# Linear attention into a mish layer: one more group in seven products, and decayed keys on GpSimd

## The chip, the cores and the metric

The kernel runs on one core of a Trainium2 chip. The metric is the device time of one execution in microseconds. The kernel before takes 207.13 us (median of three runs, 207.11 to 207.51).

## What is computed

Two stages follow one another: a causal linear attention with a decay for each head, and a two-layer block with a mish activation. In the reference, cut to what matters:

```python
# q, k, v: (4, 8, 768, 64); lam: (8,); w_in: (512, 2048); w_out: (2048, 512)
for b in range(nb):                              # blocks of 64 positions
    intra = (q_b @ k_b^T * Dmask) @ v_b          # Dmask: lam^(i-j) for i >= j, else 0
    inter = (q_b * lam^(pos+1)) @ kv_state
    out_b = intra + inter
    kv_state = lam^64 * kv_state + (k_b * lam^(63-pos))^T @ v_b
x = out as (3072 tokens, 512)
h = x @ w_in
g = h * tanh(log(1 + exp(h)))                    # mish
return g @ w_out                                 # (3072, 512) float32
```

Inputs and output are float32; the kernel works in float16 with float32 sums.

## The kernel before

The kernel uses blocks of 128 positions, so the sequence of 768 gives six groups, numbered 0 to 5 in the code; "fourth group" is number 3. A group holds the same 128 positions of all four batches: 512 tokens. Three things are done for a group: its attention (batch by batch, b = 0 to 3), its first layer (x by w_in, then mish into `hsg`), and its second layer (`hsg` by w_out, stored).

The order of all instructions is written out by hand (a manual schedule), one list for each engine, and each engine takes its list in order. The middle of the kernel is a loop over periods n = 1 to 4. Period n does the second layer of group n in fourteen halves, called by `h(1)`; the first layer of group n + 1; and the attention of group m = n + 2 as long as there is one. So the keys of groups 3 and 4 are decayed in periods 1 and 2; in period 3, group 5, the last, needs no state and so no decayed keys.

The attention of a batch has two calls. `s_(b)` does the decayed keys `kd` (`decay_k`, L244: keys by `lk`) and the scores on TensorE (L251), masked on VectorE into `sb` (L255). `o_(b)` does the outputs on TensorE (L271, L276), scaled on VectorE into `xn` (L279) and transposed by a DMA into `xt`; then the state: products of `kd` and values on TensorE (L297), added to the old state on VectorE into `raw` (L305), and decayed on GpSimd into the new state `w` (L307). `fetch` has GpSimd issue the loads of the next group (L87).

The first layer is done in one of two ways, by a letter in `KINDS[n]` for each of its four parts. A "p" part is four plain units, `u(ni)`: four matmuls of 512 columns each (L324), then mish (L330). An "s" part is a set: one step of Strassen's scheme, which gets four quarter blocks from seven products (`seven`, L407) of four matmuls of 256 columns. It needs sums of w_in (`w_sum`, L370, four operations for each set, called by `ws(n, i)` through the table `WSUMS`), sums of x (`x_sums`, L385), two copies on ScalarE (L421, L429) and two additions on VectorE (L432, L436, the second into `c22`). Its steps are m1, seed, m2, m5, m6, m7, m3 and m4; `settle()` runs the m4 that `closing` left owed. The second layer has its own sums of `hsg` (`sums`, `gsum`, L481) on VectorE. The tile `kd` has three buffers; `kn`, `qn` and `vn` have four.

Of the kernel before, what the change touches and what calls it, by code (L numbers as in the profile page):

```python
# [20 lines left out]
def kernel(  # L21
# [10 lines left out]
    nc = tc.nc  # L32
# [209 lines left out]
    def decay_k(n, b, eng):  # L242
        kd[n, b] = work.tile([128, H, D], F16, name="kd", tag="kd", bufs=3)
        eng.tensor_tensor(out=kd[n, b], in0=kn[n, b], in1=bc(lk, 2, D), op=ALU.mult)  # L244
# [549 lines left out]
    def h(m=1):  # L794
        for _ in range(m):
            halves.pop(0)()
# [2 lines left out]

    KINDS = {1: "pppp", 2: "pppp", 3: "ssss", 4: "ssss"}
    WSUMS = {(1, 0): (0,), (1, 1): (2,), (2, 0): (1,), (2, 1): (3,)}

    for n in range(1, NG - 1):
        m = n + 2
        last = m >= NG - 1

        def u(*units):
            for ni in units:  # L810
                unit(n + 1, ni, next_bank())

        def s_(b):
            if m < NG:
                if not last:
                    decay_k(m, b, nc.vector)
                scores(m, b)

        def o_(b):
# [10 lines left out]
        def ws(n, i):  # L830
            for x in WSUMS.get((n, i), ()):
                for t in range(4):
                    w_sum(x, t, nc.vector)

        kinds = KINDS[n]
        sets = []
# [72 lines left out]
        if kinds[0] == "s":  # L909
            h(1)  # L910
            mm(0, "m2", "m5", "m6")
            sums(n, 1, 0, 1)
            h(1)
            o_(0)
            fetch(("k", 0), ("q", 0))
            closing(0)
        else:
            u(0)
            sums(n, 1, 0, 1)
            if n == 1:  # L920
                weight_sum(3, 0)
                weight_sum(3, 1)
            h(1)
            u(1)
            h(1)
            u(2)
            o_(0)
            fetch(("k", 0), ("q", 0))
            u(3)


        opening(1)
        h(1)
        if kinds[1] == "s":
            settle()
            mm(1, "m2")
            h(1)
            mm(1, "m5", "m6")
            sums(n, 1, 2)
            h(1)  # L940
            o_(1)
            fetch(("v", 0), ("k", 1))
            closing(1)
        else:
            u(8)
            settle()
            s_(1)
            sums(n, 1, 2, 3)
            ws(n, 0)
            h(1)  # L950
            u(9, 10)
            o_(1)
            fetch(("v", 0), ("k", 1))
            h(1)
            u(11)


# [6 lines left out]
        if kinds[2] == "s":  # L964
            mm(2, "m2", "m5", "m6")
            o_(2)
            fetch(("q", 1), ("v", 1))
            h(1)
            closing(2)
            h(1)  # L970
            sums(n + 1, 0, 0, 1)
            h(1)
        else:
            u(4)
            settle()
            s_(2)
            u(5)
            ws(n, 1)
            h(1)
            u(6)  # L980
            o_(2)
            fetch(("q", 1), ("v", 1))
            h(1)
            sums(n + 1, 0, 0, 1)
            h(1)
            u(7)
# [3 lines left out]
        if kinds[3] == "s":  # L990
            h(1)
            mm(3, "m2", "m5")
            h(1)
            mm(3, "m6")
            o_(3)
            h(1)
            mm(3, "m7", "m3")
            owed.append(3)
            sums(n + 1, 0, 2, 3)
        else:  # L1000
            s_(3)
            h(1)
            u(12)
            settle()
            h(1)
            o_(3)
            u(13)
            sums(n + 1, 0, 2, 3)
            h(1)
            u(14)  # L1010
# [46 lines left out]
```

## Time and profile before

| what | value |
|---|---|
| median of three runs | 207.13 us |
| the profiled execution's own time | 207.71 us |
| its span, first to last instruction | 205.8 us |
| busy: PE (TensorE) | 195.8 us, 95% |
| busy: DVE (VectorE) | 142.5 us, 69% |
| busy: ACT (ScalarE) | 95.9 us, 47% |
| busy: POOL (GpSimd) | 70.7 us, 34% |
| kd on DVE (L244) | 20 times, mean 741 ns |
| state decay on POOL (L307) | 14 times, mean 1456 ns |
| granted TensorE clock | 0.995 |

All times are from one execution, taken by the hardware profiler. PE is the row of matmuls, PEld that of weight loads, which overlap it. A row of a timeline gives the start in us from the span's start, the length, the engine, the line of the kernel, the operation and "output<-inputs" with shapes; behind it, in brackets, stands the idle time of the engine ahead of the instruction and what ended it. "x4" at the end counts merged instructions. Matmuls are pipelined, so the distance between the starts of two groups tells more than a group's length, which contains the last one's run out of the array.

### The profile page before, as it was taken

The numbers are of one execution on the slowest core, as the hardware profiler recorded it, in microseconds if no ns is written. First come the engines' busy times: TensorE is split into PE (matmuls) and PEld (weight loads), VectorE is DVE, ScalarE is ACT, GpSimd is POOL, SyncE is SP. The second block draws the span as 40 slices with busy tenths as digits, with TensorE's granted clock in tenths as the row PEclk, the third lists the DMA queues.
The fourth block names the chain that finished last, engine by engine and source line by source line (L and its number), as shares of the span: only waits on it lengthen the run. The fifth ranks groups of instructions, "written<-read, shape, count | busy, mean of one in ns | idle before, by whom it ended". The sixth has DMA issues, their size and how long they took to land.

```text
span 205.8 us, 4537 instructions
## 1 busy us (share of the span) xinstructions
PE 195.8 (95%) x1879; PEld 145.1 (70%) x1879; DVE 142.5 (69%) x241; ACT 95.9 (47%) x170; POOL 70.7 (34%) x68
## 2 busy tenths in 40 slices
PE   7968998999999999999999999999999999999991
PEld 3755554688865556667666567668888988888891
DVE  6656749777766957779965779977588676269041
ACT  4674686648631115243255342255574474827300
POOL 7996553533272560744630744530000000000020
PEclk9999999999999999999999999999999999999998
DMA  9999999999969999799994399992212221003123
GB/s 130 133 168 206 163 181 157 175 207 185 136 117 147 242 135 211 109 126 103 196 226 99 77 133 135 191 245 65 56 26 76 62 69 54 2 0 105 51 102 102
DMA packets 109302, 26.24 MB, mean 128 GB/s; under 512 B 99426, under 2 KB 108770, under 8 KB 109282
## 3 DMA queue, kind: packets, MB, share of 16 engines
q0 software_dynamic: 77536, 13.37, 83.8%
q1 hardware_dynamic: 30704, 12.33, 28.2%
q10 hardware_dynamic: 1042, 0.26, 0.6%
q8 instruction: 14, 0.23, 0.4%
q14 instruction: 6, 0.05, 0.1%
HBM read 27.26 MB, written 6.29 MB: 163 GB/s over the span
## 4 chain that ended last, share of the span: by engine, by line
PE 78%; DMA 9%; POOL 8%; DVE 1%; ACT 1%; issue 1%; POOLq 0%; DVEq 0%; ACTq 0%
PE bG L518 15%; PE bH L518 13%; DMA qn<-in_q_dram 8%; PE bA L324 5%; PE bC L324 5%; PE bB L324 4%; PE bB L407 3%; PE bC L407 3%; PE be L251 3%; PE bB L350 3%; PE bA L407 2%; PE bA L350 2%; PE bC L350 2%; POOL win L96 2%; PE bz L276 2%; PE bz L271 2%
## 5 line engine op out<-in xcount | busy, mean ns | idle before, releaser
L307 POOL TENSOR_TENSOR w<-raw,lbm 128x512 f16<-128x512 f32 x14 | 20.4, 1456 | 53.0 <-DVE raw L305 49.9
L518 PEld LDWEIGHTS <-gsum 128*128 128x128 f16 x336 | 31.1, 98 | 5.1
L324 PEld LDWEIGHTS <-win 128*128 128x128 f16 x200 | 18.3, 98 | 14.6 <-issue 1.0
L518 PEld LDWEIGHTS <-hsg 128*128 128x128 f16 x240 | 23.3, 98 | 5.6
L255 DVE TENSOR_TENSOR sb<-be,dm 128x512 f16<-128x512 f32 x23 | 15.8, 686 | 15.0 <-PE bo L251 15.0
L600 POOL TENSOR_TENSOR c<-p,u 128x512 f32<-128x512 f32 x1 | 1.3, 1275 | 61.2 <-DVE p L599 61.2
L518 PE MATMUL bH<-tsum,gsum 128*128 128x256 f16 x160 | 20.4, 273 | 0.0
L279 DVE TENSOR_TENSOR xn<-bz,lq 128x512 f16<-128x512 f32 x20 | 13.7, 686 | 9.3 <-PE bz L276 9.3
L518 PE MATMUL bG<-wout,hsg 128*128 128x256 f16 x160 | 20.1, 273 | 0.0
L324 PE MATMUL bA<-xt,win 128*128 128x512 f16 (+2 forms) x72 | 17.6, 367 | 0.6 <-ACT xt L265 0.6
L330 ACT ACTIVATE hsg<-bA 128x512 f16<-128x512 f32 x17 | 10.2, 597 | 13.9 <-PE bA L324 13.9
L324 PE MATMUL bC<-xt,win 128*128 128x512 f16 x64 | 16.4, 379 | 0.0
L330 ACT ACTIVATE hsg<-bB 128x512 f16<-128x512 f32 x15 | 9.0, 598 | 14.6 <-PE bB L324 14.6
L255 DVE TENSOR_TENSOR sb<-bo,dm 128x512 f16<-128x512 f32 x23 | 15.6, 679 | 0.0
L324 PE MATMUL bB<-xt,win 128*128 128x512 f16 (+2 forms) x64 | 15.6, 366 | 0.0
L481 DVE TENSOR_TENSOR gsum<-hsg 128x1024 f16<-128x1024 f16 x20 | 14.9, 751 | 0.0
L330 ACT ACTIVATE hsg<-bC 128x512 f16<-128x512 f32 x16 | 9.6, 597 | 11.4 <-PE bC L324 11.3
L244 DVE TENSOR_TENSOR kd<-kn,lk 128x512 f16<-128x512 f16 x20 | 14.6, 741 | 0.0
L350 PEld LDWEIGHTS <-win 128*128 128x128 f16 x128 | 12.1, 98 | 1.8
L407 PEld LDWEIGHTS <-wsum 128*128 128x128 f16 x128 | 12.4, 98 | 1.4
L87 POOL DMA_DIRECT2D kn<-in_k_dram x10 | 11.8, 1182 | 2.8 <-PE bo L297 1.4
L87 POOL DMA_DIRECT2D vn<-in_v_dram x10 | 11.6, 1160 | 2.6 <-DMA win<-in_moe_w_in_dram 1.8
(161 smaller groups left out, 393.1 us busy)
## 6 DMA issues: line engine op xcount, KB each, us to landing
out_dram<-osum SPq DMA_DIRECT2D x23, 256.0 KB, 2.4
kn<-in_k_dram POOLq DMA_DIRECT2D x11, 256.0 KB, 7.3
qn<-in_q_dram POOLq DMA_DIRECT2D x11, 256.0 KB, 6.8
vn<-in_v_dram POOLq DMA_DIRECT2D x10, 256.0 KB, 8.1
wout<-in_moe_w_out_dram POOLq DMA_DIRECT2D x4, 512.0 KB, 15.9
win<-in_moe_w_in_dram POOLq DMA_DIRECT2D x3, 512.0 KB, 11.5
vz<-in_v_dram POOLq DMA_DIRECT2D x2, 256.0 KB, 6.5
k<-in_k_dram SPq DMA_DIRECT2D x1, 256.0 KB, 3.3
```

The source lines that it names most:

```text
L87: nc.gpsimd.dma_start(out=tile_, in_=rows(src, n, 2 * bp, 2))
L244: eng.tensor_tensor(out=kd[n, b], in0=kn[n, b], in1=bc(lk, 2, D), op=ALU.mult)
L251: nc.tensor.matmul(p_[t][:, j, :], kT[n, b][rs, j, :], qT[n, b][rs, j, :], start=True, stop=True)
L255: nc.vector.tensor_tensor(out=sb[n, b, t], in0=p_[t], in1=dm[:, t], op=ALU.mult)
L279: nc.vector.tensor_tensor(out=xn, in0=po, in1=bc(lq, 2, D), op=ALU.mult)
L307: decay = lambda: eng.tensor_tensor(out=w_new, in0=raw, in1=lbm, op=ALU.mult)
L324: nc.tensor.matmul(open_[n, ni][:, lo:hi], win[ni // 4][:, kc, (ni % 4) * 128 : (ni % 4) * 128 + 128], xt[n][:, kc, lo:hi], start=(opens a ...
L330: nc.scalar.activation(h_tile(n)[:, ni, :], open_.pop((n, ni)), AF.Mish)
L350: nc.tensor.matmul(t[:, u, :], win[ni // 4][:, kc, m : m + 128], xt[n][:, kc, cs], start=(u == 0 and kc == 0), stop=(kc == NKC - 1), skip_ ...
L407: nc.tensor.matmul(t[:, u, :], lhs, rhs, start=(fresh and u == 0 and kk == 0), stop=(kk == 1), skip_group_check=True)
L481: nc.vector.tensor_tensor(out=gsum[n, i][:, ks, :], in0=a, in1=b, op=op)
L518: nc.tensor.matmul(t, lhs(kk, blk), rhs(kk)[:, lo:hi], start=(fresh and kk == 0), stop=(kk == HK - 1), skip_group_check=True)
```

## The change

Three edits go together.

First, period 2's letters become "ssss": the first layer of group 3 is done in four sets, as that of groups 4 and 5 is already. Group 2's stays plain.

Second, the sums of w_in, which were made two sets in period 1 and two in period 2, are all made in period 1, and the places of the calls in the plain branch move. (The calls in that branch run in period 1 alone now.)

Third, `decay_k` inside the loop goes from VectorE to GpSimd: eight operations, four in each of periods 1 and 2.

```diff
-    KINDS = {1: "pppp", 2: "pppp", 3: "ssss", 4: "ssss"}
-    WSUMS = {(1, 0): (0,), (1, 1): (2,), (2, 0): (1,), (2, 1): (3,)}
+    KINDS = {1: "pppp", 2: "ssss", 3: "ssss", 4: "ssss"}
+    WSUMS = {(1, 0): (0,), (1, 1): (2,), (1, 2): (1,), (1, 3): (3,)}
...
                 if not last:
-                    decay_k(m, b, nc.vector)
+                    decay_k(m, b, nc.gpsimd)
                 scores(m, b)
...
             fetch(("k", 0), ("q", 0))
             u(3)
+            ws(n, 0)
...
             sums(n, 1, 2, 3)
-            ws(n, 0)
             h(1)
             u(9, 10)
             o_(1)
             fetch(("v", 0), ("k", 1))
             h(1)
+            ws(n, 1)
             u(11)
...
             u(5)
-            ws(n, 1)
-            h(1)
+            h(1)
+            ws(n, 2)
             u(6)
...
             settle()
+            ws(n, 3)
             h(1)
             o_(3)
```

GpSimd's list in period 1, batches 0 to 2, before: the state decay of a batch, then two loads.

```order
L307 TENSOR_TENSOR w_414<-raw,lbm 128x512
L87 DMA kn<-in_k_dram 128x16x64
L87 DMA qn<-in_q_dram 128x16x64
L307 TENSOR_TENSOR w_429<-raw,lbm 128x512
L87 DMA vn<-in_v_dram 128x16x64
L87 DMA kn<-in_k_dram 128x16x64
L307 TENSOR_TENSOR w_460<-raw,lbm 128x512
```

The same place after:

```order
+L244 TENSOR_TENSOR kd<-kn,lk 128x512
 L307 TENSOR_TENSOR w_414<-raw,lbm 128x512
 L87 DMA kn<-in_k_dram 128x16x64
 L87 DMA qn<-in_q_dram 128x16x64
+L244 TENSOR_TENSOR kd<-kn,lk 128x512
 L307 TENSOR_TENSOR w_429<-raw,lbm 128x512
 L87 DMA vn<-in_v_dram 128x16x64
 L87 DMA kn<-in_k_dram 128x16x64
+L244 TENSOR_TENSOR kd<-kn,lk 128x512
 L307 TENSOR_TENSOR w_460<-raw,lbm 128x512
```

The decayed keys of a batch now stand behind the state decay and the two loads of the batch before it. In period 2 it is the same.

VectorE's list in period 1 from the outputs of batch 0 to those of batch 1, before (w_414 is the state of batch 0, wsum_150 the sums for the first set):

```order
L279 TENSOR_TENSOR xn<-bz,lq 128x512
L305 TENSOR_TENSOR raw<-be,w_414 128x512
L244 TENSOR_TENSOR kd<-kn,lk 128x512
L255 TENSOR_TENSOR sb<-be,dm 128x512
L255 TENSOR_TENSOR sb<-bo,dm 128x512
L481 TENSOR_TENSOR gsum_1222<-hsg 128x1024
L481 TENSOR_TENSOR gsum_1224<-hsg,gsum_1184 128x1024
L370 TENSOR_TENSOR wsum_150<-win_71 128x512
L370 TENSOR_TENSOR wsum_150<-wsum_150,win_71 128x512
L370 TENSOR_TENSOR wsum_150<-win_71 128x512
L370 TENSOR_TENSOR wsum_150<-win_71,wsum_150 128x512
L279 TENSOR_TENSOR xn<-bz,lq 128x512
```

And after:

```order
L279 TENSOR_TENSOR xn<-bz,lq 128x512
L305 TENSOR_TENSOR raw<-be,w_414 128x512
L370 TENSOR_TENSOR wsum_150<-win_71 128x512
L370 TENSOR_TENSOR wsum_150<-wsum_150,win_71 128x512
L370 TENSOR_TENSOR wsum_150<-win_71 128x512
L370 TENSOR_TENSOR wsum_150<-win_71,wsum_150 128x512
L255 TENSOR_TENSOR sb<-be,dm 128x512
L255 TENSOR_TENSOR sb<-bo,dm 128x512
L481 TENSOR_TENSOR gsum_1222<-hsg 128x1024
L481 TENSOR_TENSOR gsum_1224<-hsg,gsum_1184 128x1024
L279 TENSOR_TENSOR xn<-bz,lq 128x512
```

`kd` has left, and the four sums of w_in stand right behind `raw`, ahead of the masks. Likewise the next four now come right behind the next `raw`, and the last two times four ahead of `xn` of batches 2 and 3.

VectorE's list in period 2, batches 0 and 1, after; what was there before were kd, masks, sums of w_in and gsum, with no L385, L432 or L436:

```order
L432 TENSOR_TENSOR bC<-bB,p_1742 128x512
L481 TENSOR_TENSOR gsum_1548<-hsg 128x1024
L481 TENSOR_TENSOR gsum_1550<-gsum_1548,hsg 128x1024
L279 TENSOR_TENSOR xn<-bz,lq 128x512
L305 TENSOR_TENSOR raw<-be,w_414 128x512
L436 TENSOR_TENSOR c_1795<-bB,p_1742 128x512
L255 TENSOR_TENSOR sb<-be,dm 128x512
L255 TENSOR_TENSOR sb<-bo,dm 128x512
L432 TENSOR_TENSOR bB<-bC,p_1857 128x512
L481 TENSOR_TENSOR gsum_1642<-hsg 128x1024
L279 TENSOR_TENSOR xn<-bz,lq 128x512
L305 TENSOR_TENSOR raw<-be,w_429 128x512
```

The set's two additions now frame the outputs and the state of each batch, and `raw` stands between `xn` and the second of them.

## The prediction

> **What bounds the kernel now.** I read the windows first, then the chain that ended last, then the timelines of TensorE, GpSimd and VectorE through the two periods that the change touches. The windows cut the middle of the kernel at the first instruction of periods n = 1, 2 and 3. The columns are the stretch, its length, then busy time and count for PE, PEld, DVE, ACT and POOL.
>
> ```profile
> 77.03:107.53 30.50, 30.50 (x273) 20.52 (x272) 24.95 (x41) 11.93 (x20) 12.71 (x10) 1.00 1.59 159
> 107.53:137.98 30.45, 30.45 (x274) 20.61 (x273) 23.55 (x39) 11.93 (x20) 12.72 (x10) 1.00 1.31 148
> 137.98:165.80 27.82, 27.82 (x304) 24.13 (x302) 20.76 (x36) 14.46 (x26) 0.00 (x0) 1.00 0.26 66
> ```
>
> PE is busy for all of each period. It takes its instructions in order, and nothing there waits; so what is taken from PE's work is gained in full, and any wait put into PE's queue is lost in full. VectorE has 5 to 7 us of slack per period, GpSimd 18. The chain says the same: pieces of PE work end to end. Two of them price the change (start, length, four matmuls each):
>
> ```profile
> 79.27 0.86 PE bA L324 x4
> 139.91 0.44 PE bA L407 x4
> ```
>
> **What is taken off PE.** In period n = 2 sixteen units of four matmuls (L324, 16 x 0.86 = 13.76 us) become four sets of seven steps of four matmuls (L407, 28 x 0.44 = 12.32 us). That is 1.44 us less by these rounded rows. The windows check it: period 3 already works in sets and is 2.63 us shorter than period 2, but it lacks the four state products L297. Each is 0.23 us, the distance of these two starts:
>
> ```profile
> 82.16 0.39 PE L297 MATMUL be<-vn,kd 128*128 128x128 f16 x4
> 82.39 1.03 PE L324 MATMUL bC<-xt,win 128*128 128x512 f16 x4
> ```
>
> That is 0.92 together, which leaves 1.71. I take 1.6, between the two.
>
> **What the sets add beside PE.** On ACT eight copies, on VectorE eight additions and four x_sums:
>
> ```profile
> L421 ACT ACTIVATE bB<-bA 128x512 f32<-128x512 f32 x4 | 2.3, 587 | 0.0
> L432 DVE TENSOR_TENSOR bC<-bB,p 128x512 f32<-128x512 f32 x4 | 2.8, 699 | 6.9 <-PE bB L407 5.4 <-ACT p L429 1.5
> L385 DVE TENSOR_TENSOR xsum<-xt,xsum 128x512 f16<-128x512 f16 x4 | 1.7, 421 | 0.1
> 140.18 0.60 PE L407 MATMUL bC<-xsum,wsum 128*128 128x256 f16 x4
> ```
>
> Period 3 carries the same and PE did not wait, so I cost them at nothing, with one exception (step F). The cover is its 27.82 us of PE work; with that gone each addition is 0.7 us on PE. x_sums stand first in VectorE's queue in period 2 and wait there for the last transposed block. The first product that needs one comes 2.2 us into a period (137.98 to 140.18); a block that lands later than that is lost time, which period 3 did not show.
>
> **The sums of w_in.** Sixteen operations stay sixteen; eight move from period 2 to period 1, and all change place within period 1.
>
> ```profile
> 95.00 0.42 DVE L370 TENSOR_TENSOR wsum<-wsum,win 128x512 f16<-128x512 f16 x1
> 95.34 0.42 DVE L370 TENSOR_TENSOR wsum<-win 128x512 f16<-128x512 f16 x1
> ```
>
> From start to start each is 0.34. Period 1 loses four kd (0.6 each, 82.97 to 83.57 below) and gains eight of these: 0.3 us more work on VectorE, with 5.5 idle. As neighbours of GpSimd they matter more, as the next rows show.
>
> **What moves to GpSimd.** Here is GpSimd in period 1 before, then PE's other state products, then VectorE (the last row groups all kd: shortest, median and longest ns).
>
> ```profile
> 83.74 1.64 POOL L307 TENSOR_TENSOR w<-raw,lbm 128x512 f16<-128x512 f32 x1 [8.36 <-DVE raw L305]
> 85.33 1.21 POOL L87 DMA_DIRECT2D kn<-in_k_dram  x1
> 86.53 1.15 POOL L87 DMA_DIRECT2D qn<-in_q_dram  x1
> 90.75 1.26 POOL L307 TENSOR_TENSOR w<-raw,lbm 128x512 f16<-128x512 f32 x1 [3.07 <-DVE raw L305]
> 91.97 1.20 POOL L87 DMA_DIRECT2D vn<-in_v_dram  x1
> 93.17 1.15 POOL L87 DMA_DIRECT2D kn<-in_k_dram  x1
> 97.38 1.26 POOL L307 TENSOR_TENSOR w<-raw,lbm 128x512 f16<-128x512 f32 x1 [3.06 <-DVE raw L305]
> 103.59 1.64 POOL L307 TENSOR_TENSOR w<-raw,lbm 128x512 f16<-128x512 f32 x1 [2.65 <-DVE raw L305]
> ```
> ```profile
> 88.48 0.39 PE L297 MATMUL be<-vn,kd 128*128 128x128 f16 x4
> 95.67 0.39 PE L297 MATMUL be<-vn,kd 128*128 128x128 f16 x4
> 102.00 0.39 PE L297 MATMUL be<-vn,kd 128*128 128x128 f16 x4
> ```
> ```profile
> 82.97 0.68 DVE L305 TENSOR_TENSOR raw<-be,w 128x512 f32<-128x512 f32 x1
> 83.57 0.68 DVE L244 TENSOR_TENSOR kd<-kn,lk 128x512 f16<-128x512 f16 x1
> 97.81 1.38 DVE L481 TENSOR_TENSOR gsum<-hsg 128x1024 f16<-128x1024 f16 x1
> 103.43 0.68 DVE L481 TENSOR_TENSOR gsum<-hsg 128x1024 f16<-128x1024 f16 x1
> 104.03 1.76 DVE L481 TENSOR_TENSOR gsum<-hsg,gsum 128x1024 f16<-128x1024 f16 x1
> L244 DVE TENSOR_TENSOR kd<-kn,lk x20: 677/682/1762, 17.3 to 130.4; 128x512 f16<-128x512 f16 x20
> ```
>
> First reading: two clients, one door. L307 takes 1.26 us alone and 1.64 when a VectorE operation with two SBUF inputs (kd at 83.57, gsum at 103.43) is under way as it starts. A gsum that starts while L307 runs takes 1.38 or 1.76 instead of 0.68, and ends 0.68 after L307's end. Whoever starts second waits for the whole of the other. Every kd on GpSimd can so be held for up to one VectorE operation (0.6 us) and can hold gsum, weight sums and x_sums for 1.27.
>
> Second reading: a loop. In the new order kd of batch b+1 stands on GpSimd behind L307 and the two DMA issues of batch b. L307 needs raw, raw needs PE's state product of batch b, and PE's state product of batch b+1 needs that kd. On VectorE kd hung on none of this. The loop, from state product to state product: to the start of L307 1.58 us (82.16 to 83.74) when VectorE is free and 2.27 (88.48 to 90.75) when it is not; to the end of the second DMA issue 3.57 (90.75 to 93.17 plus 1.15); kd itself; and a handoff of 0.1 (83.65, raw's end, to 83.74).
>
> The price of kd on GpSimd has no row before. Ends: 0.68, what it takes on VectorE, and 1.76, the longest of its rows, one that was blocked. I take 1.27, the nearest row: L307 is the same operation on the same engine with as many elements. Then the loop is 6.52 to 7.21 us. The Trainium skill, in its page "GPSIMD Engine Reference", sections "Performance versus the Vector engine" and "Engine selection", puts a two-input operation at about 2.6 cycles per element at 1.2 GHz and calls VectorE the place for ordinary elementwise work. By that page kd would be an estimated 1.11 us, four stalls would each be 0.16 shorter and the forecast below 0.6 lower; the trace's 1.26 for the like operation decides.
>
> PE's spacing of state products in period 1 is 6.32, 7.19 and 6.33 us by their rows (82.16, 88.48, 95.67, 102.00). In period 2 it is read off period 3's order, where outputs (L271) stand as they will:
>
> ```profile
> 141.93 0.39 PE L271 MATMUL bz<-w,qT 128*128 128x128 f16 x4
> 148.50 0.39 PE L271 MATMUL bz<-w,qT 128*128 128x128 f16 x4
> 153.32 0.39 PE L271 MATMUL bz<-w,qT 128*128 128x128 f16 x4
> 161.63 0.39 PE L271 MATMUL bz<-w,qT 128*128 128x128 f16 x4
> ```
>
> With one state product of 0.23 more in each interval: 6.80, 5.05 and 8.54. The first kd of each period costs nothing: in period 1 GpSimd sat idle for 8.36 us ahead of 83.74, and in period 2 the kd follows the L307 of 103.59, some 6 us ahead of its product, which stands about 4 us into a period that begins at 107.53 (141.93 against 137.98).
>
> **Step A, period 1, batch 1.** L307 waits for one weight sum rather than kd and ends about 85.2; DMA issues to 87.5. VectorE, held by L307 to 85.2, has three weight sums (0.34) and two score masks (0.6) to do and reaches a gsum at 87.5. If the gsum has the door, kd runs 88.1 to 89.4; PE wanted it at 88.48: 0.95 lost. (If kd is first: 0.45, and the second gsum then delays batch 2 by the rest.)
> **Step B, batch 2.** PE wants it at 95.67 + 0.95 = 96.6. raw ends at 91.2, L307 behind a weight sum at 92.85, DMA issues at 95.2, kd at 96.45: nothing.
> **Step C, batch 3.** That kd holds the third weight sums, which now stand ahead of xn and raw, to 96.45; they end at 97.8, raw at 99.0, L307 at 100.35, DMA issues 102.7, kd 104.0. Wanted at 102.00 + 0.95: 1.1 lost.
> **Step D, period 2, batch 1.** Two gsums stand ahead of raw, so the long loop, 7.2, against 6.80: 0.45.
> **Step E, batch 2.** A loop of some 6.75 (1.8 to L307, as the held gsum delays xn) against 5.05: 1.7. Batch 3 has 8.54: nothing.
> **Step F, the set's own addition.** c (L436) is read by the set's step m4 on PE. In period 3 it made it like this:
>
> ```profile
> 144.03 0.68 DVE L436 TENSOR_TENSOR c<-bB,p 128x512 f32<-128x512 f32 x1
> 149.82 0.68 DVE L436 TENSOR_TENSOR c<-bC,p 128x512 f32<-128x512 f32 x1
> 145.00 0.60 PE L407 MATMUL bB<-xsum,win 128*128 128x256 f16 x4
> 150.69 0.61 PE L407 MATMUL bC<-xsum,win 128*128 128x256 f16 x4
> ```
>
> It ends 0.29 and 0.19 us ahead. In period 2 raw, 0.6, stands before it, and PE has only 0.23 more to do: 0.1 and 0.2, so 0.3.
>
> Sum: 0.95 + 1.1 + 0.45 + 1.7 + 0.3 = 4.5 lost, 1.6 gained, 2.9 us slower. Nothing after period 2 takes it back, since PE is the chain to the end. The profiled execution took 207.71 us (span 205.8 and 1.9 around it), 0.58 above the median of 207.13; against the median, 210.0. Ends: with every loop at its shortest and the door always free A and C are 0.2 each and E 1.05 to 1.46 (1.05 if xn was done during the stall): 1.45 to 1.85 lost, 0.15 faster to 0.25 slower. With kd at 0.68 the steps lose about 2.3, so +0.7; with kd at 1.76 each of four stalls grows by 0.49, so +4.9.
>
> **Rivals.** A change under 0.2% (0.41 us) cannot be told from none.
> Only step E remains: the queues happen to meet without the door. For it: L307 met no VectorE operation in two of four batches. Against: weight sums and gsums now stand just where GpSimd starts. 207.0 to 207.4.
> Kd is never late, and the gain comes whole: 205.5. That needs GpSimd to run kd beside its own DMA issues, at least 1.7 us before the second one's row ends, for it decides at step E. For: PE sees kd only by its semaphore, and GpSimd's spans are rough. Against: the small operation behind a DMA issue at the kernel's start began only when the issue had ended:
>
> ```profile
> 4.69 1.14 POOL kn L82
> 5.83 0.28 POOL ek L123
> ```
>
> VectorE becomes the bound in period 2: it held 20.76 us in period 3, plus four raw of 0.68 is 23.5, plus eight holds of 1.27 at most 33.6, above PE's 28.7 to the worth of 4.9: 212 or more. Against: the holds fall mostly in its idle gaps.
> That the sets save less than 1.6 in period 2 is excluded by period 3's row, but for waits counted above.
>
> **How the numbers follow.** Forecast, +1 to +4.5: 0.66. Only E: 0.14, all of it no change. Kd never late: 0.14, faster. VectorE the bound: 0.06. So faster 0.14, same 0.14, slower 0.72. The range reaches from the case of only E, 207.0, to a kd near its upper end, 211.5; outside lie the faster case and the worst one. The forecast's own range is 208.1 to 211.6.
>
> **What would show it.** PE waits on POOL kd L244 ahead of L297 in both periods, longest at batch 2 of period 2 (1 to 2 us), small or none at batch 2 of period 1; kd rows on GpSimd near 1.27 or 1.65; period 1 about 32.5 us instead of 30.50, period 2 about 31.2 instead of 30.45. It is wrong if kd rows start before the DMA rows end, if kd is nearer 0.7, or if PE is fully busy in period 2 at 28.7.

## The result

The changed kernel takes 209.5 us (median of six runs, 208.96 to 210.13); the kernel before 207.32 us (six runs, 206.95 to 207.94). The ratio is 1.0079, with a 95% interval of 1.0052 to 1.0107: slower by 0.8% (the two medians alone would give 1.0105, inside the interval). One execution of a later run took 404 us and one of another 694 us; the ratios leave these two out. The profiled execution of the changed kernel took 209.33 us, with a span of 207.5 us; that of before 207.71, with a span of 205.8. So the two traces differ by 1.6 to 1.7 us, the medians by 2.2, and the forecast was 2.9. Every number below that comes from a trace is one execution's.

First the windows, cut within 0.1 us of the start of periods 1, 2 and 3 (stretch, its length, then busy time and count of PE, PEld, DVE, ACT and POOL):

```profile
76.60:108.40 31.80, 30.75 (x274) 20.61 (x273) 29.97 (x46) 11.91 (x20) 16.39 (x14) 1.00 1.55 154
108.40:139.40 31.00, 29.25 (x323) 25.46 (x321) 25.21 (x39) 14.61 (x28) 16.05 (x14) 1.00 1.27 131
139.40:167.50 28.10, 28.05 (x305) 24.15 (x303) 21.23 (x37) 15.37 (x28) 0.00 (x0) 1.00 0.32 79
```

PE is no longer busy for all of periods 1 and 2: 1.05 and 1.75 us are missing. VectorE was busy for 24.95 us in period 1 before; now it is 29.97, although four kd have left it and only eight short sums have come. The rest is time in which it stood held inside its operations. The view of TensorE's waits between 74 and 172 us names the gaps. For the kernel before it has no row at all; now it has these (output, line, what it waited for: us in total, times, longest):

```profile
PE bH L518 <- DVE u L546: 1.1, 1, 1.1
PE be L297 <- POOL kd L244: 0.9, 1, 0.9
PE be L251 <- DVE raw L305: 0.7, 1, 0.7
PE bC L407 <- DVE c L436: 0.2, 1, 0.2
```

And TensorE's timeline shows where each of them stands, with the idle time in brackets:

```profile
94.44 1.03 PE L518 MATMUL bH<-tsum,gsum 128*128 128x256 f16 x8 [1.05 <-DVE u L546]
115.28 0.21 PE L251 MATMUL be<-qT,kT 64*128 64x128 f16 x1 [0.68 <-DVE raw L305]
122.65 0.60 PE L407 MATMUL bC<-xsum,win 128*128 128x256 f16 x4 [0.18 <-DVE c L436]
126.78 0.40 PE L297 MATMUL be<-vn,kd 128*128 128x128 f16 x4 [0.89 <-POOL kd L244]
```

Of four waits one is for kd on GpSimd. The largest is for `u`, an addition on VectorE that the change does not touch. The bracket counts only part of a loss, so I measure losses by the distance of PE starts, after against before. The state products (L297) give period 1; the quoted rows of before stood at 88.48, 95.67 and 102.00:

```profile
88.22 0.40 PE L297 MATMUL be<-vn,kd 128*128 128x128 f16 x4
96.63 0.39 PE L297 MATMUL be<-vn,kd 128*128 128x128 f16 x4
103.06 0.39 PE L297 MATMUL be<-vn,kd 128*128 128x128 f16 x4
120.44 0.39 PE L297 MATMUL be<-vn,kd 128*128 128x128 f16 x4
```

From the second state product to the third it is 8.41 us instead of 7.19: the wait for `u`, 1.22. From the third to the fourth it is 6.43 instead of 6.33. In period 2 the same method, with the distances of period 3 for the sets, gives 0.76 for `raw`, 0.22 for c and 1.06 for kd, 2.04 in all. The table measures each period from its first PE instruction to that of the next; period 3 is measured to the second product of period 4 (0.44 behind the first) in every run:

| | period 1 | period 2 | period 3 | sum |
|---|---|---|---|---|
| before | 30.50 | 30.45 | 28.48 | 89.43 |
| after | 31.79 | 30.99 | 28.68 | 91.46 |
| difference | +1.29 | +0.54 | +0.20 | +2.03 |

Where a period starts matters a little: scores, with which periods 1 and 2 began before, start 0.96 us after the products ahead of them, and m1, with which period 2 begins now, 0.87. Counted alike, period 2 took 30.54 before, and period 1 now loses 1.38 (1.22, 0.10, and 0.06 at its second state product). Period 2 without its 2.04 of waits would be 28.95, that is 1.59 shorter: the gain that was forecast at 1.6. Ahead of period 1 the trace of after happens to be 0.33 earlier, which brings the difference of the two spans to 1.7.

### The profile page after: what moved, and what is told of

Same layout as the page of the kernel before. It is cut to its first block, busy times and chain, and to the rows that moved or that the text cites. A ratio compares the mean times of both kernels' runs of the same rounds, so it can differ in the third digit from the quotient of the medians.

```text
span 207.5 us, 4668 instructions
## 1 busy us (share of the span) xinstructions
PE 193.8 (93%) x1927; PEld 148.9 (72%) x1927; DVE 150.0 (72%) x245; ACT 99.4 (48%) x178; POOL 78.8 (38%) x76
## 4 chain that ended last, share of the span: by engine, by line
PE 75%; DVE 8%; DMA 4%; ACT 4%; POOL 4%; issue 3%; POOLq 0%; DVEq 0%; ACTq 0%
PE bG L518 13%; PE bH L518 12%; PE bB L407 5%; PE bA L324 4%; PE bC L407 4%; PE bB L324 3%; PE bA L407 3%; DMA qn<-in_q_dram 3%; PE bC L324 3%; DVE wsum L370 3%; PE be L251 3%; PE bB L350 3%; PE bA L350 2%; PE bC L350 2%; PE bz L276 2%
## 5 line engine op out<-in xcount | busy, mean ns | idle before, releaser
L307 POOL TENSOR_TENSOR w<-raw,lbm 128x512 f16<-128x512 f32 x14 | 19.5, 1393 | 48.1 <-DVE raw L305 48.1
L407 PEld LDWEIGHTS <-wsum 128*128 128x128 f16 x192 | 18.6, 98 | 2.1
L324 PEld LDWEIGHTS <-win 128*128 128x128 f16 x136 | 12.2, 98 | 10.2 <-issue 1.0
L407 PEld LDWEIGHTS <-win 128*128 128x128 f16 x144 | 13.8, 98 | 2.6 <-issue 0.6
L350 PEld LDWEIGHTS <-win 128*128 128x128 f16 x128 | 12.1, 98 | 1.8
L87 POOL DMA_DIRECT2D qn<-in_q_dram x10 | 11.6, 1164 | 1.8 <-PE bo L297 0.9
L411 ACT ACTIVATE hsg<-bC 128x512 f16<-128x512 f32 x10 | 5.9, 594 | 13.2 <-PE bC L407 13.2
L407 PE MATMUL bA<-xt,win 128*128 128x256 f16 x80 | 12.0, 272 | 0.1
L324 PE MATMUL bA<-xt,win 128*128 128x512 f16 (+2 forms) x48 | 11.5, 361 | 0.6 <-ACT xt L265 0.6
L330 ACT ACTIVATE hsg<-bA 128x512 f16<-128x512 f32 x11 | 6.6, 597 | 10.1 <-PE bA L324 9.9
L324 PE MATMUL bC<-xt,win 128*128 128x512 f16 x44 | 11.3, 379 | 0.0
```

What stands on the lines that cost most here:

```text
L87: nc.gpsimd.dma_start(out=tile_, in_=rows(src, n, 2 * bp, 2))
L307: decay = lambda: eng.tensor_tensor(out=w_new, in0=raw, in1=lbm, op=ALU.mult)
L324: nc.tensor.matmul(open_[n, ni][:, lo:hi], win[ni // 4][:, kc, (ni % 4) * 128 : (ni % 4) * 128 + 128], xt[n][:, kc, lo:hi], start=(opens a ...
L330: nc.scalar.activation(h_tile(n)[:, ni, :], open_.pop((n, ni)), AF.Mish)
L350: nc.tensor.matmul(t[:, u, :], win[ni // 4][:, kc, m : m + 128], xt[n][:, kc, cs], start=(u == 0 and kc == 0), stop=(kc == NKC - 1), skip_ ...
L407: nc.tensor.matmul(t[:, u, :], lhs, rhs, start=(fresh and u == 0 and kk == 0), stop=(kk == 1), skip_group_check=True)
```

## The experiments

The three parts of the change were taken apart first, then single places were moved, then a version was looked for that keeps the gain. All ratios are to the kernel before, run beside each on the same chip, the experiments in five rounds each. The last four columns are worked out as in the table above, from one trace each.

| run | ratio | 95% interval | period 1 | period 2 | period 3 | sum |
|---|---|---|---|---|---|---|
| changed kernel | 1.0079 | 1.0052 to 1.0107 | 31.79 | 30.99 | 28.68 | 91.46 |
| changed, kd on VectorE | 1.0002 | 0.9980 to 1.0025 | 30.84 | 30.32 | 28.93 | 90.09 |
| before, kd on GpSimd | 1.0088 | 1.0068 to 1.0107 | 31.37 | 31.27 | 28.48 | 91.12 |
| before, sums in period 1 | 1.0002 | 0.9975 to 1.0029 | 30.93 | 30.71 | 28.48 | 90.12 |
| changed, kd a step early | 1.0060 | 1.0042 to 1.0078 | 31.68 | 30.02 | 29.43 | 91.13 |
| changed, kd ahead of loads | 1.0079 | 1.0055 to 1.0104 | 31.44 | 30.30 | 29.65 | 91.39 |
| changed, sums spread | 1.0111 | 1.0094 to 1.0129 | 31.27 | 30.98 | 28.67 | 90.92 |
| reordered, kd on VectorE | 0.9985 | 0.9960 to 1.0010 | 30.41 | 30.31 | 28.82 | 89.54 |
| reordered, kd early | 1.0031 | 1.0004 to 1.0057 | 30.41 | 30.44 | 28.81 | 89.66 |
| kd ahead of x_sums | 0.9983 | 0.9964 to 1.0002 | 30.41 | 29.92 | 28.82 | 89.15 |
| the same without that | 1.0003 | 0.9976 to 1.0030 | 30.40 | 30.26 | 28.84 | 89.50 |
| raw and c first | 0.9986 | 0.9956 to 1.0015 | 30.41 | 30.38 | 29.43 | 90.22 |
| seed first | 1.0003 | 0.9970 to 1.0037 | – | – | – | – |

(As above, a period that ends with a set's product instead of scores measures 0.09 shorter. Hence 30.41 in period 1 is a period without any loss, but for "kd on GpSimd" and "sums in period 1", where it is 30.50; and period 2 is compared with 30.54, but for these two, where it is 30.45.)

### Kd back on VectorE

```diff
                 if not last:
-                    decay_k(m, b, nc.gpsimd)
+                    decay_k(m, b, nc.vector)
```

> The changed kernel with the decayed keys back on VectorE; the sets and the moved sums of w_in stay. Theory (GpSimd's kd costs by its place behind two loads, and by holding the shared door against VectorE's two-input operations): PE's wait for kd at batch 2 of period 2 (0.9 to 1.1 us) is gone, and the third weight sum behind L307, which took 1.26 us in the changed kernel, takes 0.42, so that the wait of PE for u (1.05) shrinks to 0.4 or less; the waits for raw and for c in period 2 stay, perhaps 0.3 longer as VectorE has kd again. Time 1.3 to 1.9 us below the changed kernel, 0.2 to 0.8 above the kernel before. Rival (VectorE is overfull in period 1 by eight more weight sums, and kd on GpSimd relieves it): time above the changed kernel by 0.5 us or more, PE waits for u of over 1.2 us. Second rival (a load's issue on GpSimd holds the door by itself): the third weight sum still takes about 1.26.

207.67 us; the ratio is 1.0002 and no difference from before can be told (0.2 to 0.8 us above it was expected), against 1.0079 with kd on GpSimd. The move of kd is worth about 1.6 us, and all that made the change slower. TensorE's waits in the same stretch are now

```profile
PE be L251 <- DVE raw L305: 0.7, 1, 0.7
PE bz L276 <- DVE sb L255: 0.3, 1, 0.3
PE bH L518 <- DVE u L546: 0.2, 1, 0.2
PE bC L407 <- DVE c L436: 0.2, 1, 0.2
```

The waits for kd and for `u` in period 1 are gone together (the small one for `u` is in period 2). Those for `raw` and c stay, so kd on GpSimd has no part in them. But period 2 is only 0.22 shorter than before, in place of 1.59: with kd on it, VectorE is 27.46 us busy there of 30.32, and the sets' gain is lost in pieces. Period 1 loses 0.43, at the masks of its last batch.

### Kd alone on GpSimd

```diff
 # in the kernel before
-                    decay_k(m, b, nc.vector)
+                    decay_k(m, b, nc.gpsimd)
```

> The kernel before with its third edit alone: decayed keys of periods 1 and 2 on GpSimd, everything else as before. Theory: the loop from state product to state product with kd of 1.06 us measured is 6.3 to 7.0 us, against a spacing on PE of 6.32, 7.19 and 6.33 in both periods: PE waits for kd of 0 to 0.4 us at batches 1 and 3, none at 2; weight sums do not stand behind raw, so no wait for u. 0 to 1.0 us above the kernel before. Rival (the wait for kd comes from GpSimd's own slowness and not from the spacing of the sets): PE waits of about 1 us at several batches, 2 us or more above the kernel before. Second rival (kd off VectorE is a plain gain): 0.3 us or more below the kernel before.

209.26 us, 0.9% and 1.8 us slower: more than expected, and as much as the whole change loses. Here is its view of waits, and two of its kd rows; those that nothing holds take 1.06:

```profile
PE be L297 <- POOL kd L244: 0.6, 2, 0.3
PEld L276 <- DVE sb L255: 0.4, 2, 0.2
```
```profile
86.94 1.60 POOL L244 TENSOR_TENSOR kd<-kn,lk 128x512 f16<-128x512 f16 x1
94.81 1.06 POOL L244 TENSOR_TENSOR kd<-kn,lk 128x512 f16<-128x512 f16 x1
```

The waits for kd name 0.6, but periods 1 and 2 are 0.87 and 0.82 longer. By the distances of the state products the second is 0.47 late in either period, the third 0.15 and the fourth 0.25. The second waits for a kd that a gsum held at the door (1.60), and the third starts 0.06 behind a kd's end (95.87 and 95.93), although no row of waits names it. The fourth is late by the masks, which stand on VectorE behind two held gsums. So kd on GpSimd costs without any set, by the prediction's loop and door together, and partly through operations that are not kd.

### The sums of w_in alone

```diff
 # in the kernel before
-    WSUMS = {(1, 0): (0,), (1, 1): (2,), (2, 0): (1,), (2, 1): (3,)}
+    WSUMS = {(1, 0): (0,), (1, 1): (2,), (1, 2): (1,), (1, 3): (3,)}
 # and the calls of ws at the changed kernel's places
```

> The kernel before with its second edit alone: all sums of w_in in period 1, at the changed kernel's places; group 3's first layer plain, decayed keys on VectorE. Theory: VectorE's list of period 1 is that of the run with kd back on VectorE and the sets, where PE waited 0.26 us for the masks of batch 3 and for nothing else in period 1; so 0 to 0.5 us above the kernel before. Rival (the moved sums are a good part of the loss): 0.8 us or more above it.

Ratio 1.0002 (0.9975 to 1.0029): nothing that can be told. The trace has a wait of 0.26 for masks in period 1 (0.43 by the distance of the state products, as in the first run) and one of 0.23 for a transposed block at the start of period 2, so the move is not quite free, but it is no cause by itself. The first run had these sums and the sets and comes to the same ratio, so the sets add nothing to them, neither loss nor gain.

### Kd one step earlier, ahead of the state decay

```diff
-                if not last:
+                if not last and b == 0:
                     decay_k(m, b, nc.gpsimd)
 # in o_, ahead of the state of batch b
+                if not last and b < 3:
+                    decay_k(m, b + 1, nc.gpsimd)
```

> The changed kernel with each kd on GpSimd one batch earlier: that of batch b+1 ahead of the state decay of batch b, so that it stands behind no load that waits for that batch. Theory: PE's wait for kd at batch 2 of period 2 (0.9 to 1.1 us) is gone; the wait for u in period 1 stays at about 1.0, as the same kd still comes behind the same loads and holds the door at the same time; waits for raw (0.7) and c (0.2) stay. 0.8 to 1.2 us below the changed kernel. Rival (the wait there is only the last of several; raw or the masks come next): less than 0.4 us below.

208.72 us, ratio 1.0060 against 1.0079: some 0.4 us better by the ratios, where 0.8 to 1.2 was expected. No wait for kd is left, and period 2 falls by 0.97 to 30.02, so the wait's 1.06 was real. But `u` still waits for 1.1, and period 3 grows from 28.68 to 29.43. Its start shows why, in VectorE's timeline:

```profile
140.36 0.43 DVE L385 TENSOR_TENSOR xsum<-xt 128x512 f16<-128x512 f16 x1 [1.89 <-DMA xt<-xn]
```

The sums of x wait for the last transposed block. TensorE came there 1.06 earlier than in the changed kernel, and the first of these sums only 0.16. The masks and the first addition stand behind it on VectorE, and TensorE loses 0.7 to these two. So 0.75 of what period 2 won came back in period 3.

### Kd behind the state decay, ahead of the loads

```diff
 # in o_, behind the state of batch b and ahead of fetch
+                if not last and b < 3:
+                    decay_k(m, b + 1, nc.gpsimd)
```

> The changed kernel with the decayed keys of batch b+1 on GpSimd right behind the state decay of batch b and ahead of its two loads, instead of behind them. Theory (the idle part of GpSimd starts kd while the loads are still being issued, and holds the door from then; the part that issues does its share afterwards, when the door is held again): the third weight sum behind L307 is still held, 1.2 to 1.3 us, now beside a kd row; the gsum that took 1.01 us at the end of the loads in the changed kernel takes 0.68 to 0.7; PE's wait for kd at batch 2 of period 2 is gone; the wait for u stays near 1.0. 0.7 to 1.2 us below the changed kernel. Rival (a load's issue holds the door when a weight sum comes behind a held one, kd has no part in it): the third weight sum is free (0.42) or is held beyond the end of kd until the first load's issue ends.

209.53 us, ratio 1.0079, no better than the changed kernel, where 0.7 to 1.2 us less was expected. Again no wait for kd, and `raw` now waits for 1.0 and `u` for 0.8. Period 2 is 30.30, period 3 29.65: what is won in the two periods is given back at the start of the third. The two DMA issues in the loop are thus not the only price of kd on GpSimd. It still holds VectorE at the door: a sum of 0.41 takes 1.26 beside its row (the last section shows it).

### The sums of w_in spread out again

```diff
-    WSUMS = {(1, 0): (0,), (1, 1): (2,), (1, 2): (1,), (1, 3): (3,)}
+    WSUMS = {(1, 0): (0,), (1, 1): (2,), (1, 3): (3,), (2, 1): (1,)}
 # calls of ws(n, 0) and ws(n, 1) where they stood before
```

> The changed kernel with the sums of w_in at other places: the first two sets' back behind the gsums and the masks where the kernel before had them, the third set's in period 2 behind the masks of batch 1, the fourth's where the change put it; kd stays on GpSimd. Theory: PE's wait for u in period 1 (1.05) is gone, the waits in period 2 for raw, c and kd stay (0.7, 0.2, 0.9), with at most 0.3 more from the four weight sums there. 0.7 to 1.2 us below the changed kernel. Rival (u is late because VectorE as a whole lags, not because the door is held just there): the wait moves to another VectorE product in period 1 and the time falls by less than 0.4.

The wait for `u` is gone, which shows that it hung on the sums ahead of it; kd now waits 1.2 in two places, one of them in period 1 as the prediction had it. The time is 209.76 us, ratio 1.0111, no better than the changed kernel, although PE's periods are 0.54 shorter in the trace and its last matmul ends 0.6 earlier. There the last output waited 2.12 us for a store in front of it (0.90 in the changed kernel, 1.35 before). All four runs took 209.68 to 209.92 us, so the time repeats, but one trace can't tell whether that wait does; this miss stays open.

### Reordered, with kd on VectorE

```diff
 # from "kd back on VectorE": in o_, raw ahead of xn
-                outputs(m, b)
-                if not last:
-                    state(m, b, "e", nc.gpsimd)
+                outputs(m, b, between=None if last else lambda: state(m, b, "e", nc.gpsimd))
 # in opening(2) of a set, u ahead of the gsum
-            sums(n, 1, 3)
-            h(1)
+            h(1)
+            sums(n, 1, 3)
 # and the sums of w_in spread as in the run above
```

> The sets of period 2 with the decayed keys on VectorE, and VectorE's list reordered: raw ahead of xn, u ahead of the last gsum of period 2's second batch, the sums of w_in of two sets back at the places of the kernel before and those of the third in period 2. Theory (the gain of 1.6 us is there, and what is left against it are single late operations on VectorE): PE's waits for raw (0.7), the masks (0.3) and u (0.2) fall to 0.1 each or less, that for c (0.2) stays; 0.7 to 1.1 us below the kernel before, ratio 0.9945 to 0.9970. Rival (VectorE is full at period 2's start, so that an operation put ahead makes another late): waits of 0.7 us or more at other VectorE products, within 0.4 us of the kernel before.

207.55 us, ratio 0.9985 (0.9960 to 1.0010): not shown faster, and short of what the theory expected. Period 1 loses nothing. Period 2 still loses 1.36 of 1.59: `raw` 0.4, c 0.4, and the rest in pieces.

### The same with kd on GpSimd, one step early

```diff
-                if not last:
-                    decay_k(m, b, nc.vector)
+                if not last and b == 0:
+                    decay_k(m, b, nc.gpsimd)
 # in o_, ahead of the state of batch b
+                if not last and b < 3:
+                    decay_k(m, b + 1, nc.gpsimd)
```

> The run before this one, with the decayed keys on GpSimd, each one batch early and so off the loop. Theory (kd on GpSimd costs by the loop and by the door): the loop's waits are gone, the door's holds stay, and weight sums no longer stand right behind L307; PE waits of 0.3 us or less for kd, and together 0 to 0.7 us above the reordered kernel with kd on VectorE. Rival (with the loop gone GpSimd relieves VectorE): below it by 0.3 us or more.

208.31 us, ratio 1.0031 (1.0004 to 1.0057): slower than before by a little, and 0.5% above its twin with kd on VectorE (the two intervals just overlap), without one row in which TensorE waits for kd. The waits are for `raw` 0.5, c 0.4 and bC of the next set 0.4, all of them VectorE's. So even in the best place found for it kd on GpSimd shows no gain. That it costs there is not shown: the two traces are 0.7 us of span apart (206.3 and 205.6), of which the three periods hold 0.12, and 0.5 lies behind the start of the last output (202.72 and 202.49).

### Three more moves on VectorE

The first run moves the first kd of period 2 into idle time ahead of the sums of x, takes xn first in the last batch and puts a gsum behind the block that it followed; the second leaves the kd where it was.

```diff
+            if not last:
+                decay_k(m, 0, nc.vector)
             x_sums(n + 1, 0, 1, 2, 3)
 # o_(3): xn first again; opening(2)'s sums(n, 1, 2) behind closing(1)
```

> The kernel of the run with the keys decayed on VectorE and the reordered sums, with three moves more: the decayed keys of the fifth group's first batch stand ahead of the sums of x on VectorE (in the idle time in which these wait for the transposed block), the last batch of a period takes xn ahead of raw again, so that the transposes start earlier, and the third set's sum for period 2 stands behind the last block of period 1. Theory (what is left of the gain is lost where VectorE is late at three places, and these have idle time ahead of them): TensorE's waits for raw (0.45) and c (0.41) fall to 0.1 or less, the start of period 3 loses 0.1 to 0.2 in place of 0.34, and the time is 0.8 to 1.2 us below the kernel before (ratio 0.994 to 0.997). Rival (VectorE is full in period 2, and each wait taken away comes back at another row): within 0.4 us of before.

> The same without the first of the three moves: the decayed keys of the fifth group's first batch stay where they were. Theory: the wait for raw stays near 0.45, that for c falls; 0.3 to 0.8 us below the kernel before. Rival (VectorE full): within 0.3 us of before, and the same as its companion.

207.28 us, ratio 0.9983 (0.9964 to 1.0002), and 207.85 us, ratio 1.0003 (0.9976 to 1.0030). Both theories missed and the rivals held: within 0.4 us of before. In the first VectorE is busy for 27.06 of the 29.93 us of period 2 (its windows, then TensorE's waits):

```profile
107.66:137.59 29.93, 29.20 (x322) 25.38 (x322) 27.06 (x46) 15.05 (x28) 11.97 (x10) 1.00 1.39 144
```
```profile
PE bC L409 <- DVE c L438: 0.4, 1, 0.4
PE be L251 <- DVE raw L307: 0.3, 1, 0.3
```

Its period 2 is 0.62 shorter than before, 0.97 short of the 1.59, and its period 3 is 0.34 longer.

### Raw and c ahead of gsum and xn

```diff
-            sums(n, 1, 0, 1)
+            sums(n, 1, 0)
 ...
             closing(0)
+            sums(n, 1, 1)
 # batch 1 of period 2: xn behind c (outputs hands its end to closing)
```

> The kernel of the run with the decayed keys ahead of the sums of x, with two moves more on VectorE in period 2: in batch 0 the second gsum stands behind raw, xn and c and no longer ahead of raw; in batch 1 c stands ahead of xn. No work is added or removed. Theory (what period 2 still loses are a few tenths at places where VectorE's order is wrong, not its load): TensorE's waits for raw (0.33) and c (0.41) both fall below 0.15, period 2 loses 0.3 to 0.5 of the gain of 1.59 in place of 0.98, and the ratio to the kernel before is 0.994 to 0.9965. Rival (VectorE is full there): the time stays within 0.2 us of its parent's, ratio 0.9975 to 0.999, and the waits come back at masks, gsum or the next addition.

The two waits at which it aimed are gone, and these have come:

```profile
PE bH L525 <- DVE gsum L488: 0.7, 1, 0.7
PE bB L414 <- DVE bC L439: 0.4, 2, 0.2
```

The ratio is 0.9986 (0.9956 to 1.0015), its parent's 0.9983; in the trace periods 2 and 3 are 0.46 and 0.61 longer than the parent's. This is what the rival said: the waits come back elsewhere. VectorE has too much to do between the start of period 2 and its third batch, and what is put first there makes something else late.

### Seed ahead of the last mish

```diff
 # ScalarE's list at the start of period 3
-ACTIVATE hsg<-bC
 ACTIVATE bB<-bA
+ACTIVATE hsg<-bC
```

> The same, and at the start of period 3 ScalarE's seed of the first set stands ahead of the last mish of the set before it. Theory: the 0.2 us that the first products of period 3 lose behind that queue come back, and the ratio is 0.001 below that of its companion, 0.993 to 0.9955. Rival: the sums of x, which wait for the transposed block, hold the next product just as long, and the two are the same within 0.2 us.

207.99 us, ratio 1.0003 (0.9970 to 1.0037), where 0.993 to 0.9955 was expected, and by these intervals no better than its companion; 0.2 us is too little for them to tell. Its only trace is of the execution of 694 us, so nothing is read from it. The changed kernel's own trace does show the seed as what holds the first products there:

```profile
140.79 0.60 ACT L421 ACTIVATE bB<-bA 128x512 f32<-128x512 f32 x1
141.44 0.60 PE L407 MATMUL bA<-xt,win 128*128 128x256 f16 x4
```

The seed stands behind two mish operations of the set before, ends at 141.39, and the next product may then overwrite the bank that it read. This product comes 1.96 us after the period's first, in place of 1.76 before: the 0.20 by which period 3 is longer. What the reordered list made of it no trace shows.

No version is shown to beat the kernel before. The best, 0.9983, has an interval that just reaches 1.

## Why the prediction was right, and by what sizes it was off

The sign and the main cause hold: the change is slower, through kd on GpSimd, in periods 1 and 2, and period 2 is relieved of 1.59 of PE work. The time of 209.5 us lies inside the range. That the sum came as near is partly luck: two steps were over by 1.9 together, and a loss of 1.22 stood where none was expected. Of the signs named, TensorE's wait for kd showed in period 2 (0.89) but not in period 1, and kd's rows were 1.06, or 1.48 when held, in place of 1.27 and 1.65. The steps, by their own letters (us lost on PE):

| step | forecast | measured | what happened |
|---|---|---|---|
| work taken off PE | −1.6 | −1.59 | as forecast |
| A, batch 1 | 0.95 | 0.06 | kd took the door before gsum, not after |
| B, batch 2 | 0 | 1.22 | not kd: `u`, behind held sums |
| C, batch 3 | 1.1 | 0.10 | the kd before held no sums, so this one came in time |
| D, period 2, batch 1 | 0.45 | 0.76 | not kd: scores behind `raw` |
| E, batch 2 | 1.7 | 1.06 | kd, by the loop |
| F, c | 0.3 | 0.22 | as forecast |
| start of period 3 | 0 | 0.20 | not foreseen |

The column of measured sizes adds up to 2.03, as in the first table. The run with kd on VectorE has the waits of D and F too, so they are a price of the sets and not of kd.

**The work taken off PE.** The check by the windows had two small errors that the sum did not feel: the window of period 3 ended at 165.80, 0.22 ahead of the first product of period 4 (166.02), and period 2 began with scores (0.09). Set right, the check gives 1.58 in place of 1.71, and 1.59 was measured.

**The size of kd.** It was taken as 1.27, the state decay's row, from a range of 0.68 to 1.76. GpSimd's timeline has it, with the batch of step E:

```profile
118.89 1.06 POOL L244 TENSOR_TENSOR kd<-kn,lk 128x512 f16<-128x512 f16 x1
122.07 1.28 POOL L307 TENSOR_TENSOR w<-raw,lbm 128x512 f16<-128x512 f32 x1 [2.12 <-DVE raw L305]
123.30 1.20 POOL L87 DMA_DIRECT2D vn<-in_v_dram  x1
124.50 1.15 POOL L87 DMA_DIRECT2D kn<-in_k_dram  x1
125.66 1.06 POOL L244 TENSOR_TENSOR kd<-kn,lk 128x512 f16<-128x512 f16 x1
```

It is 1.06, or 0.21 less. The two rows differ in the types of their inputs, f16 here and f32 in L307; no run tells whether that is the reason. The Trainium skill, page "GPSIMD Engine Reference", section "Performance versus the Vector engine", had led to an estimate of 1.11 for kd, nearer the measured 1.06 than the row that the prediction took. By the page's price four stalls would each have been 0.16 shorter; the steps would still have been far from what was measured, for the reasons below.

**Step E** is the loop as it was described: 120.44 to 126.78 is 6.34, made of 1.63 to L307, 3.58 to the end of the second DMA issue, kd and a handoff. The forecast 6.75 had 0.21 too much for kd and 0.17 too much for L307's start, and the 5.05 that PE needed was 5.27, because c's wait lies in the same interval. What remains is 1.07.

**Step A** rested on the door: gsum would start at 87.5 and kd have to wait. Both rows stand in the traces of GpSimd and VectorE:

```profile
83.41 1.38 POOL L307 TENSOR_TENSOR w<-raw,lbm 128x512 f16<-128x512 f32 x1 [7.29 <-DVE raw L305]
84.73 1.21 POOL L87 DMA_DIRECT2D kn<-in_k_dram  x1
85.93 1.16 POOL L87 DMA_DIRECT2D qn<-in_q_dram  x1
87.09 1.07 POOL L244 TENSOR_TENSOR kd<-kn,lk 128x512 f16<-128x512 f16 x1
```
```profile
83.69 1.37 DVE L370 TENSOR_TENSOR wsum<-wsum,win 128x512 f16<-128x512 f16 x1
84.99 1.26 DVE L370 TENSOR_TENSOR wsum<-win 128x512 f16<-128x512 f16 x1
86.17 0.41 DVE L370 TENSOR_TENSOR wsum<-win,wsum 128x512 f16<-128x512 f16 x1
87.71 1.01 DVE L481 TENSOR_TENSOR gsum<-hsg 128x1024 f16<-128x1024 f16 x1
```

kd ran at 87.09 and it was gsum that was held, at 87.71. The reason is that VectorE came later than the step had it: the second sum was held by L307, as expected, but so was the third, at 84.99, for which the step had 0.34. The failed term is the hold of VectorE: one per batch was counted, two happened. With kd alone on GpSimd, where the sums are not at this place, a gsum does have the door first, and the second state product is 0.47 late.

**Step B** asked only whether kd would be late, and it was not. But the same two holds in batch 1 push what stands behind the sums:

```profile
90.89 1.38 DVE L370 TENSOR_TENSOR wsum<-wsum,win 128x512 f16<-128x512 f16 x1
92.19 1.26 DVE L370 TENSOR_TENSOR wsum<-win 128x512 f16<-128x512 f16 x1
93.71 0.68 DVE L546 TENSOR_TENSOR u<-bH,r 128x512 f32<-128x512 f32 x1
```

`u` ends at 94.39, and at 94.44 TensorE may write its bank. Before, it started at 92.14. With kd on VectorE the wait is gone; with the sums away from this place it is gone too: it takes both, and this is the largest loss of period 1.

**Step C** let the kd of batch 2 hold the third set's sums, and so `raw` and the next kd. That kd ran from 94.29 to 95.35, and the sums came behind it, from 95.50 on, and took 0.41 to 0.42 each. So `raw` ended at 98.24 in place of 99.0, and the next kd at 102.95 in place of 104.0. PE wanted it at 102.95 by the forecast, and its product started at 103.06.

**Step D** saw two gsums ahead of `raw` and asked what they do to the loop. They did it sooner, to the scores of batch 1, which write the bank that `raw` reads:

```profile
114.54 0.68 DVE L305 TENSOR_TENSOR raw<-be,w 128x512 f32<-128x512 f32 x1
115.14 0.68 DVE L436 TENSOR_TENSOR c<-bB,p 128x512 f32<-128x512 f32 x1
```

`raw` ends at 115.22 and the scores start at 115.28, where 114.52 would have followed from the product ahead of them. Here 0.45 became 0.76 through another reader of the same lateness. With PE that much later, kd came in time.

**The rivals.** "Only step E" and "kd is never late" fall with the ratio. What the second needed, that GpSimd works on kd beside its own DMA issues, may still be true in part (the last section); but TensorE's product waited for the end of kd's row (126.72 and 126.78). "VectorE becomes the bound" did not come about as priced (212), but it is what remains once kd is back on VectorE: in five versions period 2 loses 0.97 to 1.43 of the sets' 1.59, and all the waits named there are for VectorE. The prediction costed the additions of the sets at nothing, by period 3's row, in which VectorE has no kd, no `raw` and no sums of w_in. That cover did not carry over. It also read that a held gsum ends 0.68 after L307; its own rows give 0.55 (97.81 and 1.38 against 97.38 and 1.26), which changes no step by more than 0.13.

## What to carry to other kernels

When an operation moves to a slower engine behind that engine's own issues, draw the loop through it and compare it with the pace at which its result is wanted: here the move alone cost 1.8 us. Then look not only at who waits for the moved operation, but at every operation of the other engine that it can hold, and at what stands behind those: the largest single loss was at an addition that the change did not touch. And price a gain in the stage where it will be made, with the load that the stage will have: a wait taken away there is worth only as much as the next one allows (0.3 of 1.06 us in the trace of one run, nothing in another).

## What the runs showed that was not expected

VectorE is held by a kd on GpSimd before that kd has a row. In the changed kernel the third sum took 1.26 us at 84.99, while GpSimd's rows show only a DMA issue (84.73 to 85.94) and kd from 87.09. Two runs tell what holds it. With kd on VectorE the same sum stands beside the same DMA issue and is not held (nor with the sums alone moved, 84.96 and 0.41):

```profile
84.63 0.41 DVE L370 TENSOR_TENSOR wsum<-win 128x512 f16<-128x512 f16 x1
```
```profile
84.38 1.21 POOL L87 DMA_DIRECT2D kn<-in_k_dram  x1
85.58 1.15 POOL L87 DMA_DIRECT2D qn<-in_q_dram  x1
```

With kd ahead of the loads it is held as long as in the changed kernel, now beside a row of kd, and the gsum later is not:

```profile
84.83 1.22 POOL L244 TENSOR_TENSOR kd<-kn,lk 128x512 f16<-128x512 f16 x1
```
```profile
85.07 1.26 DVE L370 TENSOR_TENSOR wsum<-win 128x512 f16<-128x512 f16 x1
87.79 0.68 DVE L481 TENSOR_TENSOR gsum<-hsg 128x1024 f16<-128x1024 f16 x1
```

So it is shown that a DMA issue alone does not hold VectorE and that a kd queued behind one does. The length fits as well. What a row of GpSimd holds ends a steady time behind that row: a sum of w_in 0.27 (85.06 against 84.79, the end of L307), a gsum 0.55 (100.14 against 99.59 in period 1). Taken off 86.25, the end of the third sum, this leaves 85.98, or 1.19 behind L307. In batch 2 of period 2 a gsum ends at 125.07, which leaves 124.52, or 1.17 behind the end of L307 (123.35). With kd ahead of the loads the end of kd's row is 1.18 behind that of L307 (86.05 and 84.87).

```profile
123.71 1.36 DVE L481 TENSOR_TENSOR gsum<-hsg,gsum 128x1024 f16<-128x1024 f16 x1
```

The Trainium skill's page "GPSIMD Engine Reference" offers a mechanism: by its section "Instruction dispatch" each of GpSimd's cores starts the next instruction when its own share of the last is done, and by "When to use GPSIMD" a pair of cores generates a load's descriptors. The other cores would then run their share of kd during the issues, and the pair theirs behind them, at the row. That would explain two holds for one kd (84.99 and 87.71). The rows show GpSimd as one engine, so this is argued and not shown. That the hold lasts to the end of the other's operation (the sum at 83.69 ends 0.27 behind L307) agrees with the Trainium skill's page "SBUF — State Buffer", section "Who interferes with whom", where the shared port is an exclusive lock.
